# Weight-sum steps of VectorE asked ahead of the norms, and w2 steps that take the block stored first

## The chip, the cores and the metric

The kernel runs on one core of one Trainium2 chip. The metric is device time in microseconds, measured on the chip; every execution that the comparisons use is of the same (fast) state. Waits, stretches and timelines are those of one profiled execution of each kernel. The kernel before takes 1542.65 us (median of three runs, 1542.54 to 1543.26).

## The reference, cut to what matters

Two layers, each an attention with a short dilated window and a gated feed-forward, over 2048 tokens of width 1024. Both layers use the same weights.

```python
def _A_ref(x, wqkv, wo):            # 32 heads of 32, W = 8, dilation 2
    ... q, k, v from x @ wqkv; each token looks at itself and 7 earlier ones ...
def _B_ref(x, w1, w3, w2):          # F = 3584
    gate = jnp.einsum("bsd,df->bsf", x, w1)
    up = jnp.einsum("bsd,df->bsf", x, w3)
    h = _silu(gate) * up
    out = jnp.einsum("bsf,fd->bsd", h, w2)
    return out

x = A_x
x = x + _A_ref(_layernorm(x, axis=-1), A_wqkv, A_wo)
x = x + _B_ref(_layernorm(x, axis=-1), B_w1, B_w3, B_w2)
x = x + _A_ref(_layernorm(x, axis=-1), A_wqkv, A_wo)
x = x + _B_ref(_layernorm(x, axis=-1), B_w1, B_w3, B_w2)
```

## The kernel before

The tokens are worked in blocks of 512. The feed-forward of layer 0 does its first two blocks with plain products. Beside those it builds **weight sums**: ScalarE copies scaled pieces of w1, w3 or w2 into one of two staging blocks in `big`, VectorE adds and subtracts them, GpSimd stores the block to DRAM. All later feed-forward blocks read these sums back and need seven products where plain ones need eight (the scheme of Strassen).

VectorE's order is chosen while the program is built. It keeps queues of small steps, and `background` fills the time until the next fixed piece of work. The step that can start first by its estimate wins, and at a tie the queue that is asked first:

```python
def background(until):
    while True:
        best = None
        for queue in (norms, makes, adds, values, scores):
            step = head(queue)
            if step is not None:
                start = max(now["dve"] + 0.3, step[1])
                if start - 0.3 + step[0] <= until and (best is None or start < best[0]):
                    best = start, queue
        ...
```

The norms' steps are statistics and the application of the norm; each application is followed by a DMA transpose on the sync queue. `makes` holds the weight-sum steps: four VectorE steps for a block, then its stores.

Lines of the kernel before that return below: L841 is a product of Q, K, V, and L845 its evacuation (ScalarE copies a finished product out of PSUM); L712 loads wqkv; L277 is the norm's DMA transpose; L1086 is one of the seven products of the later feed-forward blocks, L1110 VectorE's sum behind it; L1394 adds to the residual. The granted clock is the share of full speed that TensorE was allowed.

```python
def differences(m, g, a, slot, r):            # sums of w1 and w3
    b = blocks[slot]
    for out, x, y in ((4, 5, 1), (1, 1, 0), (2, 4, 0), (6, 3, 2)):
        yield 0.40, r, lambda: nc.vector.tensor_tensor(b[:, out], b[:, x], b[:, y], ...)   # L928
    pending[slot] -= 1
    nc.gpsimd.dma_start(t_d[m][g][:, 4 * a:4 * (a + 1)], b[:, 0:4])                        # L931
    nc.gpsimd.dma_start(t_d[m][g][:, 8 + 3 * a:8 + 3 * (a + 1)], b[:, 4:7])                # L932
    stored[slot] = now["dve"] + 7.0

def sums_of_w2(i, f, ws, loaded):
    a = f % 2
    while "at" not in got2 or pending[a]:
        yield "blocked"
    pending[a] += 1
    b = big[:, a * 3584:(a + 1) * 3584].rearrange("p (b c) -> p b c", b=7)
    for j, (fh, hh) in ((0, (0, 0)), (2, (0, 1)), (1, (1, 0)), (5, (1, 1))):
        yield 0.61, max(loaded, stored[a], got2["at"]), lambda: nc.scalar.activation(      # L1043
            b[:, j], ws[hh][fh][:, f, :], ACTF.Copy, scale=up2[:])
    ...
    def rest():
        ... four VectorE steps ...                                                         # L1049
        pending[a] -= 1
        nc.gpsimd.dma_start(t2_d[i][:, :, f, :], b)                                        # L1052
        stored[a] = now["dve"] + 7.0
```

## Time and profile before

| | kernel before |
|---|---|
| time, median of 3 | 1542.65 us |
| span of the profiled execution | 1542.1 us |
| TensorE busy | 1521.5 us, 99% |
| TensorE busy from 500 to 600 us | 93.11 of 100 us |
| TensorE waits from 100 to 500 us | none listed |
| TensorE waits from 500 to 575 us | 6.8 us |
| TensorE waits from 575 us to the end | 5.8 us |

How to read it: 99% busy says that TensorE is the bound, and that there is little to win. The same number hides where the missing part stands. So the share is read by stretches, and the stretch that stands out is then looked at engine by engine; the prediction does this, with the lines.

### The profile page before, as it was taken

How to read it: one execution, taken by the hardware profiler on the slowest of the kernel's cores; microseconds unless marked ns; L12 is line 12 of the kernel's file. 1: busy time of each engine (PE TensorE's matmuls, PEld its weight loads, DVE VectorE, ACT ScalarE, POOL GpSimd, SP SyncE). 2: the span in 40 equal slices, each digit the busy share in tenths (PEclk: the TensorE clock that was granted, in tenths of full speed). 3: DMA queues.
4: the chain of work that ended last, by engine and by line, in shares of the span. 5: the costliest groups of instructions: out<-in, count | busy, mean ns of one | idle time of the engine just before them, and what ended most of it. 6: DMA issues, size and time to landing. Idle time of an engine off the chain costs nothing.

```text
span 1542.1 us, 25098 instructions
## 1 busy us (share of the span) xinstructions
PE 1521.5 (99%) x9595; PEld 990.2 (64%) x9634; DVE 1200.9 (78%) x2126; ACT 884.8 (57%) x1388; POOL 156.8 (10%) x308
## 2 busy tenths in 40 slices
PE   9999999999999999999999999999999999999999
PEld 7666644444444567675685756867677667686865
DVE  4689998889979678989898958799688986445345
ACT  3885476667465346555574554666557345554633
POOL 1210102121111100102101010010202000000000
PEclk9999999999999999999999999999999999999999
DMA  9887969798896899969879888798979988878885
GB/s 326 192 230 211 271 209 337 266 307 268 270 307 226 289 326 316 313 236 312 294 285 310 310 282 270 268 342 295 308 259 322 347 281 285 311 273 333 313 295 205
DMA packets 261433, 439.57 MB, mean 285 GB/s; under 512 B 73856, under 2 KB 201088, under 8 KB 245056
## 3 DMA queue, kind: packets, MB, share of 16 engines
q1 hardware_dynamic: 248464, 390.90, 77.2%
q0 software_dynamic: 12704, 46.93, 8.7%
q8 instruction: 75, 1.23, 0.3%
q14 instruction: 46, 0.38, 0.1%
q10 hardware_dynamic: 144, 0.13, 0.0%
HBM read 345.90 MB, written 67.90 MB: 268 GB/s over the span
## 4 chain that ended last, share of the span: by engine, by line
PE 55%; DVE 4%; DMA 3%; ACT 3%; issue 1%; POOL 1%; ACTq 0%; DVEq 0%; POOLq 0%
PE st L1086 29%; PE w L1235 15%; PE ps L841 6%; PE po L776 4%; DMA qkv_d<-hT 1%; DMA t_d<-big 1%; DMA kT<-qkv_d 1%; DVE tree L595 1%; DMA xnT<-xn 1%; DVE tree L515 1%; ACT sg L1297 0%; DVE tree L670 0%; ACT big L1043 0%; ACT xn L323 0%; ACT L1297 0%
## 5 line engine op out<-in xcount | busy, mean ns | idle before, releaser
L841 PE MATMUL ps<-xnT,wqkv 128*128 128x512 f16 (+1 forms) x1469 | 320.7, 379 | 3.1 <-ACT hT L845 1.8
L1086 PEld LDWEIGHTS <-early 128*128 128x128 f16 x2688 | 263.1, 98 | 39.9 <-DVE big L303 1.7
L841 PEld LDWEIGHTS <-wqkv 128*128 128x128 bf16 x1472 | 210.6, 144 | 111.6 <-issue 4.0
L1235 PE MATMUL w<-t,hT 128*128 128x512 f16 x1008 | 226.3, 379 | 1.5 <-ACT big L1255 1.2
L1086 PEld LDWEIGHTS <-late 128*128 128x128 f16 x2016 | 197.4, 98 | 33.8 <-issue 5.5
L595 DVE TENSOR_TENSOR tree<-qT,kT 128x2048 bf16<-128x2048 bf16 x128 | 156.2, 1221 | 29.0 <-DMA qT<-qkv_d 15.4
L670 DVE TENSOR_TENSOR tree<-At,vT 128x2048 bf16<-128x2048 bf16 x128 | 156.1, 1220 | 26.8 <-DMA At<-E 25.2
L515 DVE TENSOR_TENSOR tree<-tree 128x1024 bf16<-128x1024 bf16 x256 | 175.2, 685 | 0.9
L1086 PE MATMUL st<-big,early 128*128 128x256 f16 x1344 | 172.8, 273 | 1.9 <-DVE big L303 1.4
L1086 PE MATMUL st<-xnT,late 128*128 128x256 f16 x1344 | 174.2, 273 | 0.2
L1235 PEld LDWEIGHTS <-hT 128*128 128x128 f16 x1008 | 98.3, 98 | 113.6 <-issue 3.1
L1086 PE MATMUL st<-xnT,early 128*128 128x256 f16 x1344 | 165.3, 273 | 0.0
L1098 ACT COPY st<-st 128x512 f32<-128x512 f32 x84 | 48.3, 575 | 119.6 <-PE st L1086 118.8
L776 PE MATMUL po<-wo,oT 128*128 128x512 bf16 x487 | 111.6, 379 | 2.9 <-DVE x_sb L781 1.6
L1358 PE MATMUL pu<-xnT,w3t 128*128 128x512 f16 x448 | 105.8, 379 | 0.0
L1349 PE MATMUL pg<-xnT,w1t 128*128 128x512 f16 x448 | 105.8, 379 | 0.0
L1380 PE MATMUL acc<-w2t,hT 128*128 128x512 bf16 x437 | 97.8, 379 | 0.6
L1110 DVE TENSOR_TENSOR st<-st,big 128x512 f32<-128x512 f32 x84 | 58.4, 695 | 50.2 <-ACT big L1107 50.1
L845 ACT CAST hT<-ps 128x512 bf16<-128x512 f32 x96 | 54.9, 586 | 71.3 <-PE ps L841 70.2
L1297 ACT ACTIVATE sg<-st,down_scale 128x512 bf16<-128x512 f32 x126 | 86.7, 688 | 12.6 <-PE st L1086 12.1
L1086 PE MATMUL st<-big,late 128*128 128x256 f16 x672 | 87.9, 274 | 3.8 <-DVE st L1110 3.8
L776 PEld LDWEIGHTS <-oT 128*128 128x128 bf16 x512 | 50.0, 98 | 58.3 <-issue 2.6
(167 smaller groups left out, 1919.3 us busy)
## 6 DMA issues: line engine op xcount, KB each, us to landing
early<-t_d SPq DMA_DIRECT2D x84, 1024.0 KB, 6.9
late<-t_d SPq DMA_DIRECT2D x84, 768.0 KB, 6.4
t<-t_d SPq DMA_DIRECT2D x42, 1024.0 KB, 7.6
t<-t_d SPq DMA_DIRECT2D x42, 768.0 KB, 5.3
wqkv<-in_A_wqkv_dram SPq DMA_DIRECT2D x28, 1024.0 KB, 9.0
w1t<-in_B_w_dram SPq DMA_DIRECT2D x14, 1024.0 KB, 8.0
w3t<-in_B_w_dram SPq DMA_DIRECT2D x14, 1024.0 KB, 10.9
t_d<-big POOLq DMA_DIRECT2D x28, 512.0 KB, 6.0
```

Source lines behind the costliest of these rows:

```text
L515: nc.vector.tensor_tensor(b, b, buf[:, 4:8, :], op=ALU.add)
L595: V.tensor_tensor(pr, qT[:], kT[:, :, k0:k0 + TCH], op=ALU.mult)
L670: V.tensor_tensor(tm.rearrange("p w (a e) -> p w a e", a=4), At[:].rearrange("p a w e -> p w a e"), win, op=ALU.mult)
L776: nc.tensor.matmul(ps[:], lhsT=oT[:, t, j * P:(j + 1) * P], rhs=wo[:, t, hh * 512:(hh + 1) * 512], start=(t == 0), stop=(t == KT - 1))
L841: nc.tensor.matmul(ps[:], lhsT=ws[kk // KH][:, kk % KH, t::KT], rhs=xnT[:, kk, :], start=(kk == 0), stop=(kk == KT - 1))
L1086: nc.tensor.matmul(out[:, a, :], lhsT=w[:, a, blk, k, :], rhs=rhs[:, k, :], start=start and a == 0 and k == 0, stop=k == KQ - 1, skip_grou ...
L1110: nc.vector.tensor_tensor(G["D"][:], G["D"][:], su, op=ALU.add)
L1235: nc.tensor.matmul(out[:], lhsT=lhs[:, k, j * P:(j + 1) * P], rhs=w[:, k, :], start=start and k == 0, stop=k == nq - 1, skip_group_check=True)
L1297: nc.scalar.activation(sg[:], src, ACTF.Silu, scale=inv)
L1349: nc.tensor.matmul(pg[:], lhsT=w1t[:, kk, fi * P:(fi + 1) * P], rhs=xnT[:, kk, :], start=(kk == 0), stop=(kk == KT - 1))
L1358: nc.tensor.matmul(pu[:], lhsT=w3t[:, kk, fi * P:(fi + 1) * P], rhs=xnT[:, kk, :], start=(kk == 0), stop=(kk == KT - 1))
L1380: nc.tensor.matmul(acc[:], lhsT=hT[:, f, j * P:(j + 1) * P], rhs=tiles[hh][f // nq][:, f % nq, :], start=(f == 0), stop=(f == f1 - f0 - 1))
```

## The change

The intent: weight-sum steps win ties against norm steps, so that blocks are sent to DRAM sooner; and a w2 step takes whichever free block was stored first, not a fixed one. The diff also takes out a version of the V product that nothing called.

```diff
@@ background
-            for queue in (norms, makes, adds, values, scores):
+            for queue in (makes, norms, adds, values, scores):
@@ sums_of_w2
-        a = f % 2
-        while "at" not in got2 or pending[a]:
+        while "at" not in got2 or all(pending):
             yield "blocked"
+        a = min((i for i in range(2) if not pending[i]), key=lambda i: stored[i])
         pending[a] += 1
@@ (cut: dead code goes: v_products, size_of_v, sums_of_v, their tiles and DRAM
@@  buffers, and a third entry in blocks, pending and stored that only they used)
```

More of the change, by code (lines that the diff above doesn't have):

```diff
@@ L217 @@
     size2 = const.tile([P, 16], FP32, name="size2")
-    size_v = const.tile([P, 4], FP32, name="size_v")
-    down_v = const.tile([P, 1], FP32, name="down_v")
-    up_v = const.tile([P, 1], FP32, name="up_v")
     total = const.tile([P, 1], FP32, name="total")
@@ L226 @@
     h16 = hT[:].bitcast(FP16)
-    blocks += [hT[:, 9:16, :].bitcast(FP16).rearrange("p b (k c) -> p b k c", k=KT // 2)]
     t2_d = [dram.tile([P, 7, (b - a) // 2, 512], FP16, name=f"t2_d{i}") for i, (a, b) in enumerate(fsplits)]
     t_d = [[dram.tile([P, 14, KT // 2, P], FP16, name=f"t_d{m}_{g}") for g in range(NG)] for m in range(2)]
-    t_d += [[dram.tile([P, 14, KT // 2, P], FP16, name=f"t_dv_{g}") for g in range(2)]]
     qkv_d = [[dram.tile([P, KT, S], BF16, name=f"qkv_d{l}_{i}") for i in range(3)] for l in range(2)]
@@ L854, in q_part @@
             if l == 0:
-                stored[0:2] = landed, landed
+                stored[:] = landed, landed
             if first and t0 == SG:
@@ L917, in weight_sums, with differences @@
                     scale=up_scale[:, m, g:g + 1])
-            makes.append([differences(m, g, a, a, now["act"] + 0.1), None])
+            makes.append([differences(m, g, a, now["act"] + 0.1), None])
         made.add((m, g))
-    pending, stored, made, held = [0] * 3, [0.0] * 3, set(), []
+    pending, stored, made, held = [0] * 2, [0.0] * 2, set(), []
     junk = hsum[:].bitcast(BF16).rearrange("p k t -> p (k t)")
-    def differences(m, g, a, slot, r):
-        b = blocks[slot]
+    def differences(m, g, a, r):
+        b = blocks[a]
         for out, x, y in ((4, 5, 1), (1, 1, 0), (2, 4, 0), (6, 3, 2)):
@@ L929, in differences @@
                 b[:, out], b[:, x], b[:, y], op=ALU.add if (x, y) == (4, 0) else ALU.subtract)
-        pending[slot] -= 1
+        pending[a] -= 1
         nc.gpsimd.dma_start(t_d[m][g][:, 4 * a:4 * (a + 1)], b[:, 0:4])
         nc.gpsimd.dma_start(t_d[m][g][:, 8 + 3 * a:8 + 3 * (a + 1)], b[:, 4:7])
-        stored[slot] = now["dve"] + 7.0
-    got_v = {}
-    def size_of_v(i, w):
-        w_ = w[:].rearrange("p k c -> p (k c)")
-        half = w_.shape[1] // 2
-        for j in range(2):
-            yield 1.95, 40.0, lambda: nc.scalar.activation(junk, w_[:, j * half:(j + 1) * half], ACTF.Square,
-                                                           accum_out=size_v[:, 2 * i + j:2 * i + j + 1])
-        if i == 1:
-            total_scale(size_v, up_v, down_v, got_v)
-    def sums_of_v(ws):
-        while "at" not in got_v or norm_left.get(("Q", 0, NCH - 1), 1):
-            yield "blocked"
-        for g in range(2):
-            for a in range(2):
-                while pending[2]:
-                    yield "blocked"
-                pending[2] += 1
-                b = blocks[2]
-                for i, (kh, fh) in ((0, (0, 0)), (1, (0, 1)), (3, (1, 0)), (5, (1, 1))):
-                    t = 4 * g + 2 * fh + a
-                    yield 0.61, max(got_v["at"], stored[2]) + 1.0, lambda: nc.scalar.activation(
-                        b[:, i], ws[kh][:, :, t::KT], ACTF.Copy, scale=up_v[:])
-                makes.append([differences(2, g, a, 2, now["act"] + 1.0), None])
-        made.add("v")
+        stored[a] = now["dve"] + 7.0
     def finish_sums(done):
@@ L1152, in pipeline @@
             done(i)
-    def v_products(l, c):
-        key = ("Q", l, c)
-        slots, landed = [0], []
-        def stage(G, pair):
-            if ("to", pair) not in G:
-                i = slots[0] % 8 * SG
-                slots[0] += 1
-                G["to", pair] = hT[:, i:i + SG, :]
-                G["left", pair] = 2
-            return G["to", pair]
-        def consume(G, q, src, r):
-            pair, t0 = q % 2, HT * (q // 2)
-            to = stage(G, pair)
-            if q != 3:
-                nc.scalar.activation(to[:, :, t0:t0 + HT], src, ACTF.Copy, scale=down_v[:])
-                r = act(0.57, r)
-            G["left", pair] -= 1
-            G["at", pair] = max(r, G.get(("at", pair), 0.0))
-            if not G["left", pair]:
-                t = 4 * G["g"] + 2 * pair
-                nc.sync.dma_start(qkv_d[l][2][:, t:t + SG, c * CH:(c + 1) * CH], to)
-                landed.append(dma(256, G["at", pair]))
-                if len(landed) == 4:
-                    qkv_at[l, c, 2] = max(landed)
-        groups = []
-        for g in range(2):
-            G = dict(m=2, g=g, inv=down_v[:])
-            G["corner"] = lambda G=G: stage(G, 1)[:, :, HT:CH]
-            groups.append(G)
-        pipeline(key, groups, consume, lambda i: between(False, i == 0), True)
-        xnT_free[key] = now["pe"]
     def products(u, f0, f1, hold):
@@ L1399, in b_stage @@
         if u == TU - 1:
-            force(makes, lambda: not any(pending[0:2]))
+            force(makes, lambda: not any(pending))
             scale_h()
```

## The prediction

> **What bounds the kernel now.** I read the page first, then busy time by stretch, then what TensorE waited for, and then the timelines of the other engines where TensorE stood still.
>
> ```profile
> PE 1521.5 (99%) x9595; PEld 990.2 (64%) x9634; DVE 1200.9 (78%) x2126; ACT 884.8 (57%) x1388; POOL 156.8 (10%) x308
> 400.00:500.00 100.00, 99.68 (x468) 45.43 (x472) 85.81 (x174) 58.19 (x86) 16.02 (x28) 1.00 0.85 284
> 500.00:600.00 100.00, 93.11 (x581) 65.42 (x582) 74.52 (x133) 47.54 (x79) 7.57 (x12) 0.98 0.90 306
> 1400.00:1500.00 100.00, 100.00 (x761) 74.29 (x760) 45.21 (x70) 48.39 (x78) 0.00 (x0) 1.00 0.88 323
> PE st L1086 <- DVE st L1110: 3.8, 1, 3.8
> PE ps L841 <- ACT hT L845: 1.8, 1, 1.8
> PE ps L841 <- DMA wqkv<-in_A_wqkv_dram: 1.2, 2, 1.0
> 570.00:574.00 4.00, 4.00 (x25) 3.08 (x25) 4.00 (x7) 2.33 (x4) 0.00 (x0) 0.65 0.43 177
> 574.00:578.00 4.00, 4.00 (x39) 3.59 (x38) 3.85 (x8) 2.33 (x5) 0.00 (x0) 1.00 0.68 223
> ```
>
> Columns of the stretches: length, then PE, PEld, DVE, ACT, POOL busy us (instructions), granted clock, DMA share, GB/s. The reader is to see that TensorE bounds the kernel almost everywhere: from 40 to 1500 us it is busy over 97% of every stretch of 100 us, but for one, 500 to 600 us, where 6.9 us are missing. The three wait lines are all that TensorE waited for between 500 and 575 us: 3.8 + 1.8 + 1.2 = 6.8 us. The same view gives no wait at all from 100 to 500 us, and 5.8 us in small pieces from 575 us to the end. The change doesn't touch a matrix product, so it can only be worth what is in such holes. The last two stretches show a cost behind the 3.8 us hole: with the clock at 0.65, 25 matmuls were done in 4 us where the next 4 us did 39, so some (39 - 25) x 0.109 = 1.5 us more were lost (0.109 us is the spacing of these 128x256 products, 8 in 0.87 us).
>
> What makes this hole? It stands where the second block of layer 0's feed-forward ends, the last one that makes weight sums, and Q, K, V of layer 1 begin. The timelines of VectorE, GpSimd, ScalarE and SyncE there:
>
> ```profile
> 491.83 0.42 DVE L928 TENSOR_TENSOR big<-big 128x512 f16<-128x512 f16 x1 [0.39 <-ACT big L915]
> 493.37 0.75 DVE L928 TENSOR_TENSOR big<-big 128x512 f16<-128x512 f16 x2
> 498.95 0.42 DVE L928 TENSOR_TENSOR big<-big 128x512 f16<-128x512 f16 x1
> 502.80 0.41 DVE L928 TENSOR_TENSOR big<-big 128x512 f16<-128x512 f16 x1
> 504.57 1.17 DVE L928 TENSOR_TENSOR big<-big 128x512 f16<-128x512 f16 x3
> ...
> 497.65 0.22 POOL L251 TENSOR_SCALAR rstd<-mv 128x2 f32<-128x2 f32 x1 [2.46 <-DVE mv L249]
> 499.91 0.61 POOL L932 DMA_DIRECT2D t_d<-big  x1 [1.24 <-issue]
> 505.82 0.61 POOL L931 DMA_DIRECT2D t_d<-big  x1
> ...
> 513.99 5.01 ACT L1043 ACTIVATE big<-w2t,up 128x512 f16<-128x512 bf16 x8 [19.08 <-DMA wqkv<-in_A_wqkv_dram]
> 523.83 2.56 ACT L1043 ACTIVATE big<-w2t,up 128x512 f16<-128x512 bf16 x4 [4.83 <-DMA t_d<-big]
> ...
> 526.42 1.68 DVE L1049 TENSOR_TENSOR big<-big 128x512 f16<-128x512 f16 x4 [5.71 <-ACT big L1043]
> ...
> SPq L712 <- ACT big L1043: 9.5, 2, 9.4
> ```
>
> Columns: start, length, engine, line, what; in brackets the idle time before it. The eight last weight-sum steps (L928, 0.42 us each, 3.2 us of work) take from 491.8 to 505.7 us, because norm statistics and norm applications stand between them. So the second of the two blocks is sent off only at 505.8 us. ScalarE then idles 19 us before the first w2 step. The page names a wqkv load, but the matmuls of that stretch run from earlier tiles; I read the semaphores: the one it waited for last was raised at 513.8 us by the store issued at 505.82 us. That follows from the code: step f takes block f % 2, the first step here has f = 3, and block 1 is just the one stored last. Three steps over two blocks then end at 526.4 us. ScalarE, in order, evacuates Q, K, V products only after that (the 1.8 us wait), and the four wqkv loads wait for the w2 tiles it still reads (9.4 us, then the 1.2 us wait). VectorE idles 5.7 us, starts the norm sums and the attention late, and its backlog delays the sum that TensorE needs at 566 us (the 3.8 us).
>
> **What the Trainium skill says.** "TensorE: Matmul & The Clock Gate", Part 1, What's actually happening: after an idle window of about 3.4 us the array runs at half clock until it has been busy about as long. The trace agrees: the 3.80 us gap is the only one so long, and 0.65 follows it. The same page (Architectural detail) says that ScalarE and VectorE queues are strictly first-in first-out, so an emission order decides what waits behind what; the trace agrees, the evacuations start at 526.30, right behind the last w2 step. "DMA: Bandwidth & Descriptors", Anatomy of one DMA: about 2.0 us plus bytes / 436e3 us for a GpSimd-issued one, that is 4.1 us for an 896 KB w2 block; the trace has 4.9 us median for these.
>
> **The change, part by part.** (1) Dead code goes: nothing called the Strassen version of V, so its tiles and DRAM buffers cost no time. I count 0. (2) Weight-sum steps are asked before norms; at equal start times the first queue asked wins. Built and compared engine by engine, the new program has the same instructions in a new order from the first feed-forward block on. At the end of the second block the eight L928 steps stand as two unbroken fours, one before and one after the first residual addition (L1394) of the last half, and the norm statistics follow. (3) The w2 step takes the free block with the earliest store. Compared with the order change alone, this alters little else than some 25 VectorE rows at just this place; there the last four L1049 steps come before the second-last residual addition, where before ten of twelve came after the last. GpSimd's rstd steps no longer split the weight stores.
>
> Worked out at the hole (estimates from the rows above): ScalarE's last L915 ends at 492.35 + 2.56 = 494.9, four L928 take 1.6 us, so block 1 is sent off at about 497 rather than 505.8; block 0 (third and fourth step now adjacent) at about 494 rather than 499.9. A weight store took up to 8.0 us here (505.82 to 513.8), so the blocks are free at about 502 and 505. The w2 steps: block 0 at 502 to 504.5 (4 x 0.62), block 1 at 505 to 507.5, block 0 again after 1.7 us of VectorE and 4.9 us of store, at 511 to 513.6. So they end at about 513.6 rather than 526.4, 13 us earlier, before Q, K, V begin at 514.15. Then ScalarE is free for the first evacuation at 516: -1.8. The wqkv loads go at 514.5 rather than 524.6: -1.2. VectorE gets about 12 us ahead, its gather of scores stands after 80 rather than 120 products of QKV, and the backlog at 566 us should be gone: -3.8, and with it the slow clock: -1.5. Sum: **-8.3 us**. The matmuls do not change, and the last two feed-forward blocks have the same TensorE order in both programs, so what is gained in the middle stays gained.
>
> **The rivals.** First: a new wait in the same place. Norm applications for the next block now come some 5 us later (before about 506 us, after about 511), and their transposes share the sync queue with the wqkv loads; VectorE would stand in order at an L1049 if the third store is late. Six PSUM banks give TensorE about 6 x 1.73 = 10 us of slack, so I expect 0 to 3 us back. It would leave 1537. Second: the whole later schedule of attention moves, and the 5.8 us of small waits after 575 us are dealt anew; VectorE is 90% busy from 700 to 900 us, so it could become 2 or 10. That is 1530 to 1539. Third: the earlier blocks. With norms delayed in the first feed-forward block, the second could start late; but TensorE shows no wait from 100 to 500 us, and the norm steps still stand well before the block's end, so I expect nothing; if wrong, +3 to +6, some 1540. Fourth: the transfers, not VectorE, set the end of the w2 steps (DMA share is 0.90); then only half of the 8.3 comes.
>
> **Range and chances.** -8.3, with 1.3 given back for the first rival and nothing for the second: -7.0, so 1535.6. The second and third rivals make the width: 1529.5 to 1541.5. Over 2% faster would need 31 us, more than all waits of TensorE together (12.6 us after 100 us): 0.01. Over 2% slower would need a new stall of 31 us in an order that keeps every product: 0.02.
>
> **What would show it.** Right: 500 to 600 us with at most 2 us missing from TensorE; last w2 store at about 515 rather than 528.6; the L1043 idle of 19 us cut to below 8; no stretch with clock 0.65 in the middle. Wrong: the wait for L1110 still there though the w2 steps end early (then it is the attention loads that delay VectorE), or new waits after 575 us of more than 6 us beyond the old ones, or waits in 100 to 500 us.

## The result, and the profile after

The changed kernel takes **1532.26 us** (median of four runs, 1531.39 to 1534.33), beside 1542.95 us (1542.54 to 1544.27) for the kernel before. The ratio is 0.9931, with a 95% interval of 0.9914 to 0.9948. A ratio here is the mean time of one kernel's fast runs over that of the other's of the same rounds, so not quite the ratio of the medians quoted. In this kernel the line numbers are lower: L928 is now L923, L1043 is L1009, L1049 is L1015, L1052 is L1018, L1086 is L1052, L712 is L707, L303 is L298.

From the page, busy time; then stretches (columns as in the prediction); then all that TensorE waited for from 580 us on. From 500 to 580 us that view lists nothing.

```profile
PE 1518.1 (99%) x9594; PEld 989.5 (65%) x9634; DVE 1201.8 (78%) x2126; ACT 884.1 (58%) x1388; POOL 153.7 (10%) x308
500.00:600.00 100.00, 99.84 (x635) 69.56 (x637) 87.61 (x152) 49.78 (x80) 8.12 (x13) 1.00 0.88 295
570.00:574.00 4.00, 4.00 (x39) 3.58 (x37) 3.97 (x10) 2.84 (x5) 0.00 (x0) 1.00 0.78 277
PE st L1052 <- ACT big L1073: 2.2, 1, 2.2
PE st L1052 <- ACT sg L1227: 1.1, 1, 1.1
PE w L1165 <- ACT big L1185: 0.5, 1, 0.5
PE st L1052 <- ACT st L1064: 0.4, 1, 0.4
```

The hole is closed: 99.84 us of 100 are busy where it was 93.11, and the stretch at 570 us has a full clock and 39 matmuls where it had 0.65 and 25. What TensorE still waits for adds up to 4.2 us.

The timelines of VectorE, GpSimd, ScalarE and SyncE at the place of the old hole:

```profile
488.10 1.68 DVE L923 TENSOR_TENSOR big<-big 128x512 f16<-128x512 f16 x4
490.82 1.67 DVE L923 TENSOR_TENSOR big<-big 128x512 f16<-128x512 f16 x4
489.84 0.54 POOL L926 DMA_DIRECT2D t_d<-big  x1 [8.19 <-DVE big L923]
492.56 0.54 POOL L926 DMA_DIRECT2D t_d<-big  x1 [1.66 <-DVE big L923]
496.04 2.56 ACT L1009 ACTIVATE big<-w2t,up 128x512 f16<-128x512 bf16 x4 [5.53 <-DVE x_sb L1324]
506.70 2.56 ACT L1009 ACTIVATE big<-w2t,up 128x512 f16<-128x512 bf16 x4 [3.44 <-DMA t_d<-big]
512.91 0.98 POOL L1018 DMA_DIRECT2D t_d<-big  x1 [1.55 <-issue]
506.05 12.03 SPq L272 DMA_TRANSPOSE xnT<-xn  x4
518.18 2.69 SPq L707 DMA_DIRECT2D wqkv<-in_A_wqkv_dram  x4
```

The reader is to see that the eight weight-sum steps stand in two unbroken fours, 488.1 to 492.5 us, where they were spread from 491.8 to 505.7. Everything behind them moves ahead: the last weight-sum block is sent at 492.56 and not at 505.82 us, the w2 steps end at 509.3 and not at 526.4, the last w2 store leaves at 512.91 and not at 528.63, the four wqkv loads at 518.18 and not at 524.58.

To see where the 10.7 us arise, I counted weight loads of TensorE in both traces and took the time at which each kernel reaches the same one. Between the kernels this difference is 0.0 us at the start of Q, K, V of layer 1 (514 us), -9.2 us at the start of the next block's Q, K, V (710 us before, 700 us after), and -11.1 us at the end. So 9.2 us come from the stretch with the hole, and some 2 us from behind it, where the listed small waits fell from 5.8 to 4.2 us.

### The profile page after: what moved, and what is told of

It is laid out like the page before. It is cut to its first block, busy times and chain, and to the rows that moved or that the text cites. A ratio compares the mean times of both kernels' runs of the same rounds, so it can differ in the third digit from the quotient of the medians.

```text
span 1531.0 us, 25095 instructions
## 1 busy us (share of the span) xinstructions
PE 1518.1 (99%) x9594; PEld 989.5 (65%) x9634; DVE 1201.8 (78%) x2126; ACT 884.1 (58%) x1388; POOL 153.7 (10%) x308
## 4 chain that ended last, share of the span: by engine, by line
PE 97%; ACT 1%; issue 1%; DVE 0%; DMA 0%; SPq 0%; ACTq 0%
PE st L1052 32%; PE ps L836 21%; PE w L1165 16%; PE po L771 7%; PE pg L1279 6%; PE pu L1288 6%; PE acc L1310 6%; PE pq L444 1%; PE L L604 0%; DMA wqkv<-in_A_wqkv_dram 0%; ACT L629 0%; ACT L1227 0%; ACT E L629 0%; ACT sg L1227 0%; DVE x_sb L1150 0%
## 5 line engine op out<-in xcount | busy, mean ns | idle before, releaser
L1052 PEld LDWEIGHTS <-early 128*128 128x128 f16 x2688 | 262.6, 98 | 40.4 <-issue 3.5
L1052 PEld LDWEIGHTS <-late 128*128 128x128 f16 x2016 | 197.2, 98 | 30.6 <-issue 2.5
L1052 PE MATMUL st<-xnT,late 128*128 128x256 f16 x1344 | 174.2, 273 | 2.2 <-ACT big L1073 2.2
L1052 PE MATMUL st<-big,early 128*128 128x256 f16 x1344 | 172.3, 273 | 1.6 <-ACT sg L1227 1.1
L1052 PE MATMUL st<-xnT,early 128*128 128x256 f16 x1344 | 165.7, 273 | 0.0
L665 DVE TENSOR_TENSOR tree<-At,vT 128x2048 bf16<-128x2048 bf16 x128 | 156.2, 1221 | 11.9 <-DMA At<-E 10.7
L1052 PE MATMUL st<-big,late 128*128 128x256 f16 x672 | 87.1, 273 | 0.0
```

Of the source, the lines that this page charges most:

```text
L665: V.tensor_tensor(tm.rearrange("p w (a e) -> p w a e", a=4), At[:].rearrange("p a w e -> p w a e"), win, op=ALU.mult)
L1052: nc.tensor.matmul(out[:, a, :], lhsT=w[:, a, blk, k, :], rhs=rhs[:, k, :], start=start and a == 0 and k == 0, stop=k == KQ - 1, skip_grou ...
```

## The experiments

Two theories at first. **A**: the order is what counts; the late weight-sum steps delay everything behind them. **B**: the choice of block has a good share, since the w2 step waited for just the block that was stored last. A third, **C**, came out of the first runs. Each run was timed beside the kernel before on the same chip; that kernel's medians in the four batches were 1544.06, 1543.80, 1544.31 and 1543.96 us.

### First batch: each part alone

**order_only**: the kernel before with one edit.

```diff
-            for queue in (norms, makes, adds, values, scores):
+            for queue in (makes, norms, adds, values, scores):
```

> Only the queue order is changed (weight-sum steps asked before norms); step f still takes block f % 2, so at the end of the second block the first w2 step still waits for the block stored last. Theory A (mine: two causes in one chain, either one alone shortens it): block 1 is sent off at about 493 instead of 505.8 us, lands at about 501, three w2 steps end at about 514 instead of 526.4 us; the wait for the last evacuation and the slow clock go; 8 us less, 1534 +- 2. Theory B (the block choice is what counts, the order only deals the schedule anew): the hole stays, 1540 to 1543.

Measured: 1534.18 us (1533.79 to 1534.84), ratio 0.9935, interval 0.9920 to 0.9949. What TensorE waited for from 500 to 585 us; ScalarE's first two w2 steps; the four wqkv loads and the last w2 store:

```profile
PE st L1086 <- DVE st L1110: 1.3, 1, 1.3
PE ps L841 <- DMA wqkv<-in_A_wqkv_dram: 0.5, 1, 0.5
499.44 5.01 ACT L1043 ACTIVATE big<-w2t,up 128x512 f16<-128x512 bf16 x8 [10.03 <-DMA t_d<-big]
515.67 3.70 SPq L712 DMA_DIRECT2D wqkv<-in_A_wqkv_dram  x4
516.43 0.93 POOL L1052 DMA_DIRECT2D t_d<-big  x1 [4.23 <-ACT hT L845]
```

Of the 3.8 us wait 1.3 are left, and the clock stays full behind them. ScalarE still idles 10 us for the block stored last, and it costs nearly nothing. The order alone gives nearly the whole gain. The last two lines matter for theory C below: here too a w2 store leaves among the four loads, which take 12.3 us to land (median), and yet TensorE waits only 0.5 us for them.

**slot_only**: the kernel before with the other edit. The blocks of the last three w2 steps (f = 3, 4, 5) are swapped, from 1, 0, 1 to 0, 1, 0. The expectation says that nothing else moves; the traces do not bear that out. Up to 508.4 us the engines do the same work in the same order; then the first w2 step's four VectorE steps (L1049) stand at 508.5 us, where they were at 516.6, and VectorE's order differs from there on, ScalarE's from 538.7 us on, both until about 1100 us.

```diff
-        a = f % 2
-        while "at" not in got2 or pending[a]:
+        while "at" not in got2 or all(pending[0:2]):
             yield "blocked"
+        a = min((i for i in range(2) if not pending[i]), key=lambda i: stored[i])
```

> Only the block choice is changed; norms still come first. Built, this gives the same instruction order as the kernel before with the parity flipped for the last three w2 steps alone, so it acts at one place only. Theory A: the stores of the last weight sums are as late as before (499.9 and 505.8 us), so block 0 is free at about 508 and three steps end at about 520 instead of 526.4 us: TensorE does not wait for ScalarE (1.8 us gone), the wqkv wait shrinks, of the 3.8 us and 1.5 us of clock most goes; 1536.5 +- 2. Theory B: all of the gain, 1531 to 1533.

Measured: 1545.91 us (1545.16 to 1548.00), ratio 1.0012, interval 0.9997 to 1.0027. A miss for both theories. The first w2 step does start early, in pieces from 497.9 us on, and the last one ends at 524.3 us, 2 us sooner than before. Yet TensorE waits longer. Its longest wait and the stretch after it; then the last w2 step, the last two w2 stores and the loads:

```profile
PE ps L841 <- DMA wqkv<-in_A_wqkv_dram: 6.7, 2, 4.8
536.00:540.00 4.00, 3.93 (x10) 1.60 (x11) 3.59 (x6) 0.59 (x1) 0.00 (x0) 0.50 1.05 394
521.77 2.56 ACT L1043 ACTIVATE big<-w2t,up 128x512 f16<-128x512 bf16 x4 [3.01 <-DMA t_d<-big]
521.60 0.90 POOL L1052 DMA_DIRECT2D t_d<-big  x1 [9.93 <-DVE big L1049]
522.51 3.30 SPq L712 DMA_DIRECT2D wqkv<-in_A_wqkv_dram  x4
526.57 0.89 POOL L1052 DMA_DIRECT2D t_d<-big  x1 [4.06 <-ACT hT L845]
```

The wqkv loads leave 2 us earlier than in the kernel before, but between two w2 stores, and the tile that TensorE needs is there only at 536 us. The clock is at half for 6.8 us, of which 1.3 still lie in the 4.8 us gap. The first w2 store, at 510.8 us, falls onto two norm transposes in flight: they land 16.4 and 15.2 us after they were issued, where the same two took 9.4 and 8.4 us in the kernel before. The view of transfers shows the medians; from 500 to 540 us, number, KB and median us from issue to landing, first in the kernel before:

```profile
wqkv<-in_A_wqkv_dram SPq DMA_DIRECT2D x6, 1024.0 KB, 9.2
t_d<-big POOLq DMA_DIRECT2D x3, 896.0 KB, 4.9
xnT<-xn SPq DMA_TRANSPOSE x4, 6.3
```

and in slot_only:

```profile
wqkv<-in_A_wqkv_dram SPq DMA_DIRECT2D x6, 1024.0 KB, 12.9
t_d<-big POOLq DMA_DIRECT2D x3, 896.0 KB, 9.7
xnT<-xn SPq DMA_TRANSPOSE x4, 9.7
```

All three kinds take longer. The Trainium skill, "DMA: Bandwidth & Descriptors", Issuing engines are not separate DMA queues, says that transfers from the sync and GpSimd queues run on the same 16 engines and interleave there; these lines agree, since the same bytes land 3 to 5 us later here. This is **theory C**: what counts is where the w2 stores fall, against the transposes and the loads that TensorE waits for.

**both_dead_code_kept**: both edits, the dead code left in.

> Both live changes made on the kernel before, the unused Strassen-V code with its tiles and DRAM buffers kept. The instruction order is that of the changed kernel; only addresses differ. If dead code costs nothing: 1531 to 1534, the time of the changed kernel. If the addresses matter: between that and the time before.

Measured: 1532.98 us (1531.91 to 1534.09), ratio 0.9929, interval 0.9912 to 0.9945, and the waits of the changed kernel. The dead code costs nothing.

**order_first_unit_only**: the new order in the first feed-forward block alone (`stage[0]` is set to the block's number).

```diff
-            for queue in (norms, makes, adds, values, scores):
+            for queue in ((makes, norms) if stage[0] == 0 else (norms, makes)) + (adds, values, scores):
```

> The new queue order in the first feed-forward block alone, the old one elsewhere; block choice as before. The end of the second block then stands as before (eight weight-sum steps split by norms, first w2 step in the block stored last). Theory A: the hole stays and the time is that before, 1541 to 1544. Rival (the gain comes from earlier weight sums all along): half the gain or more, below 1538.

Measured: 1543.88 us (1543.10 to 1544.53), ratio 0.9997, interval 0.9982 to 1.0012. The hole stands: TensorE waits 3.1 us for L1112 (L1110 before), 1.8 us for wqkv and 1.7 us for the evacuation. So the gain is made in the second block.

### Second batch: where in the second block, and which block to take

**order_last_stage**: the new order only from the last w2 stage of the second block on.

```diff
+            for queue in ((makes, norms) if stage[0] else (norms, makes)) + (adds, values, scores):
...
+            stage[0] = u == 1 and lastsplit
```

> The new queue order only from the last w2 products of the second block on (from about 486 us), old before and in it; block choice as before. The last five weight-sum steps then stand unbroken, but one norm application comes behind all w2 steps. Theory A (what counts is when the last two weight blocks are sent off): block 1 is sent off at about 497 us, steps end at about 517, no evacuation wait, hole 1 to 4 us, 1534 to 1538. Rival (the order is needed all through the second block): 1541 to 1544.

Measured: 1539.17 us (1538.08 to 1540.36), ratio 0.9968, interval 0.9952 to 0.9985: half of the gain, just past the upper end of what was expected. The weight-sum stores leave by 497.2 us. What is left is mainly a wait for wqkv, with the clock low behind it:

```profile
PE ps L843 <- DMA wqkv<-in_A_wqkv_dram: 1.9, 1, 1.9
532.00:536.00 4.00, 4.00 (x18) 1.62 (x11) 0.69 (x1) 0.55 (x2) 0.00 (x0) 0.57 1.05 380
```

**last_stored**: the changed kernel with `max` in place of `min`, so that it takes the free block that was stored last, the wrong one on purpose.

```diff
-        a = min((i for i in range(2) if not pending[i]), key=lambda i: stored[i])
+        a = max((i for i in range(2) if not pending[i]), key=lambda i: stored[i])
```

> The changed kernel with the opposite choice: of two free blocks the one stored last. Theory A: with the weight stores issued by 493 us even the wrong block is free at about 501, steps end at about 513 us, before QKV begins: hole below 2 us, 1532 to 1535, as with the order alone. Theory B (the choice decides): the hole comes back, 1540 or more.

Measured: 1534.52 us (1533.60 to 1535.91), ratio 0.9941, interval 0.9922 to 0.9960, with no wait of TensorE from 500 to 585 us. Once the order is changed, even the worst choice of block costs no more than some 2 us. It is not the choice alone, though: the order of work differs from the changed kernel's as well, and the four wqkv loads leave at 508.71 us, before two of the transposes, where they leave at 518.18 us in the changed kernel.

**slot_moved_stores** and **before_moved_stores** test C: slot_only and the kernel before, with two of the last three w2 stores (f = 3 and 5) sent from steps of the first block instead. They are wrong on purpose, since these pieces then hold other data (the record marks these runs as correct all the same; no run tells why).

```diff
-            nc.gpsimd.dma_start(t2_d[i][:, :, f, :], b)
+            for at in {0: (0, 3), 1: (1, 5), 3: (), 5: ()}.get(f, (f,)) if i == 1 else (f,):
+                nc.gpsimd.dma_start(t2_d[i][:, :, at, :], b)
```

> The block choice alone, as in the run of it, but the stores of the first and third w2 step of the last stage (issued there at 510.8 and 526.6 us) are made in the first feed-forward block instead, from other steps' blocks: the bytes are the same, the result is wrong on purpose. Theory C (the earlier steps' stores collide with the norm transposes and the wqkv loads): transposes land by about 519 instead of 523 us, the wqkv waits of 6.7 us fall below 2.5, no half clock after them, 1533 to 1538. Rival (transfers don't matter, it is the order on VectorE or ScalarE): wqkv waits stay above 5 us, 1543 or more.

> The kernel before with the same two stores moved away (wrong on purpose). The third w2 step then needn't wait for the first one's store: steps end at about 521.5 instead of 526.4 us. Theory A: the evacuation wait of 1.8 us goes, the wqkv wait too, of the 3.8 us and its 1.5 us of slow clock at least half: 1535 to 1540. If only the first wait of 19 us matters: 1541 to 1544.

Measured: 1540.31 us (1538.92 to 1541.03), ratio 0.9974, interval 0.9958 to 0.9990; and 1544.06 us (1541.63 to 1545.20), ratio 0.9998, interval 0.9980 to 1.0016. Both are misses in time: the first lies between the ranges of C and of its rival, the second at the upper edge of "only the first wait of 19 us matters". At the hole they do what C says: of TensorE's waits from 500 to 585 us, 0.5 us are left where slot_only had 8.0, and 2.1 us where the kernel before had 6.8; neither has a half clock there. But both have a new wait for w3 near 460 us (2.9 and 2.1 us), with a half clock behind it, and reach Q, K, V of layer 1 more than 5 us late, so the totals say little.

### Third and fourth batch: the same test with the stores elsewhere

To get a total without that loss I sent the two stores at quieter times: near 378 us (**slot_stores_quiet**, **before_stores_quiet**), and, when that too made waits, during Q, K, V of layer 0 (**slot_stores_early**, **before_stores_early**; planned for 130 and 142 us, in the traces near 121 and 140 us). Their outputs are wrong, which doesn't matter for the times. The edit of the last pair; the first pair does the same behind the 16th weight-sum block:

```diff
+                at, s0 = {31: (3, 0), 34: (5, 3)}.get((c * 3 + which) * KT // SG + t0 // SG, (0, 0))
+                if at:
+                    nc.gpsimd.dma_start(t2_d[1][:, :, at, :],
+                                        big[:, 1024 * s0:1024 * s0 + 3584].rearrange("p (b c) -> p b c", b=7))
...
-            nc.gpsimd.dma_start(t2_d[i][:, :, f, :], b)
+            if (i, f) not in ((1, 3), (1, 5)):
+                nc.gpsimd.dma_start(t2_d[i][:, :, f, :], b)
```

> The choice of block alone (instruction order of slot_only), but two of its last three w2 stores, those of the first and third step (f = 3 and 5), are sent at another time: as two stores of the same 896 KB behind the 16th pair of weight stores, near 378 us, where the DMA share by stretch falls to 0.77 and then to 0. Wrong on purpose: those two w2 pieces get other contents. It repeats slot_moved_stores, whose extra stores had been put where a w3 load then landed late (near 460 us), at a quieter place. Theory C (the stores of the w2 steps collide with the norm transposes and the wqkv loads): no TensorE wait over 1 us at 500 to 585 us for wqkv, no half clock there, none near 380 or 460 us either; about 7 to 9 us faster than slot_only, so 1535 to 1539. Rival (the collision is with something else, or the +1.2 us of slot_only came from elsewhere): the 4.8 us wait for wqkv stays, time 1543 to 1546.

> The kernel before with the same two w2 stores sent near 378 us instead. Wrong on purpose. If the hole of the kernel before is made by the late weight-sum steps alone, its first waits stay and about half of it goes with the third step's wait for its store: 1537 to 1541. If transfers made the hole all by themselves, it goes whole: 1535 to 1537. If stores play no part: 1543 to 1545.

> As slot_stores_quiet, but the two moved w2 stores (896 KB each) go out during Q, K, V of layer 0, near 130 and 142 us, where the DMA share is 0.3 to 0.5 and no weight is loaded that TensorE waits for soon; the feed-forward blocks then hold two stores fewer and none more. Wrong on purpose: they carry other data. Theory C (in slot_only the w2 stores of 500 to 530 us collide with the norm transposes and the wqkv loads): no TensorE wait over 1 us from 100 to 585 us, no half clock in the middle, and now in the total too: 1534 to 1538. Rival (removing those stores is worth nothing in all): 1542 to 1546.

> The kernel before with the same two stores moved to 130 and 142 us. Wrong on purpose. The waits for L1110 (3.8 us) and the half clock behind it go, a wqkv wait of 1 to 2 us is left, nothing new arises before 500 us: 1535 to 1539. If the late weight-sum steps make the hole without the stores: 1541 to 1545.

Measured: slot_stores_quiet 1542.68 us (1542.20 to 1543.12), ratio 0.9989, interval 0.9974 to 1.0004, a miss. before_stores_quiet 1544.72 us (1543.60 to 1547.37), ratio 1.0008, interval 0.9990 to 1.0025, a miss: the range of "stores play no part". slot_stores_early 1539.20 us (1538.32 to 1539.27), ratio 0.9962, interval 0.9947 to 0.9977, 1 us past the range of C. before_stores_early 1541.50 us (1539.39 to 1542.74), ratio 0.9981, interval 0.9964 to 0.9997, past the range too, and just inside that of "the late weight-sum steps make the hole without the stores". So no total of the six runs lies in the range that was expected if the stores make the loss. The waits of TensorE, slot_stores_early from 500 to 585 us:

```profile
PE ps L841 <- DMA wqkv<-in_A_wqkv_dram: 0.4, 1, 0.4
```

and before_stores_early from 100 to 500 us (slot_stores_early waits there too, 4.7 us in all):

```profile
PE pu L1363 <- DMA w3t<-in_B_w_dram: 2.2, 1, 2.2
```

The 6.7 us for wqkv of slot_only have shrunk to 0.4, but before 500 us something is lost again. So I took every run apart at three points, by the same count of weight loads as above: how late (+) or early (-) its profiled execution reaches them, against the kernel before.

| run | at Q, K, V of layer 1 | at the next Q, K, V | between the two | at the end |
|---|---|---|---|---|
| the changed kernel | 0.0 | -9.2 | -9.2 | -11.1 |
| order_only | -1.1 | -8.1 | -7.0 | -10.0 |
| slot_only | +0.2 | +2.9 | +2.8 | +1.3 |
| slot_moved_stores | +5.3 | -2.4 | -7.7 | -4.0 |
| slot_stores_quiet | +9.0 | +0.8 | -8.2 | -0.7 |
| slot_stores_early | +5.0 | -2.8 | -7.8 | -4.6 |
| before_moved_stores | +5.4 | -0.9 | -6.3 | -0.7 |
| before_stores_quiet | +6.7 | -0.2 | -6.9 | -0.3 |
| before_stores_early | +3.2 | -4.6 | -7.7 | -4.8 |

The fourth column shows that the two stores matter. With them gone from there, all six runs win 6.3 to 8.2 us between the two points, nearly what the change wins, with the old queue order and whichever block is taken. In the traces the order of work on VectorE, ScalarE and GpSimd is the same in the three slot runs as in slot_only, and in the three before runs as in the kernel before. Nor did their late start help: counted from the start of Q, K, V, the last weight-sum store leaves 7.5 us ahead in the kernel before and 7.5 to 8.4 us ahead in the six. The second column is the price: wherever the stores were put, 3 to 9 us are lost before Q, K, V begin.

It does not show that they matter by collision. A block whose store is gone is also free at once: the third w2 step no longer waits for it (4.83 us in the kernel before, 3.01 us in slot_only). Counted from the start of Q, K, V, the w2 steps end at 4.4 to 7.8 us in the six runs, at 12.5 in the kernel before and at 10.2 in slot_only; the first of the four wqkv loads leaves at 2.6 to 6.0, 10.6 and 8.4 us. (order_only has 2.8 and the changed kernel 4.2.) The loads themselves are no faster than in the kernel before: the four take 11.7 us (median) in before_stores_early and 9.7 us there. For the kernel before, then, the traces point to the wait for the block, which is a link of the prediction's own chain; the collision shows most clearly in slot_only, where the four loads take 13.8 us. No run takes away the one and keeps the other.

What makes that loss is **open** in part. It appears near 460 us even where the stores were sent at 121 and 140 us. before_stores_early and the kernel before have the same order of work, but GpSimd's transfers take eight completion semaphores in turn, and two transfers moved ahead shift which semaphore each later one waits on. The traces show what follows next. In the kernel before, slot_only and order_first_unit_only an earlier w2 store leaves near 434 us, 8.9 to 9.0 us after a w3 load was issued, and that load lands after 13.4 to 13.9 us. In all six runs with moved stores the same store leaves only 4.1 to 5.9 us after the load, and the load lands after 15.2 to 15.7 us. ScalarE, which measures these weights, then waits 0.9 to 2.7 us for them (0 to 0.5 us in the three), starts its next w2 steps later, and the next w1 and w3 loads wait for those. That the shifted semaphores let the store go earlier fits all nine traces, but no run tests it, and this link does not account for the whole 3 to 9 us.

No version was found that beats the changed kernel. In it TensorE waits 4.2 us in all from 580 us on; 3.3 of them are two waits, 1.1 us at 668.0 and 2.2 us at 987.6 us. Just before each, ScalarE switches its function table twice, to the exponential of the attention and back (two loads of 1.28 us each, at 665.19 and 667.10 us and at 984.19 and 986.10 us). That is outside this change.

## Why the prediction was right

Predicted 1535.6 us and the same within 2%; measured 1532.26 us, inside the range of 1529.5 to 1541.5. Its steps in turn:

- **Dead code counts 0**: shown by both_dead_code_kept.
- **The hole gives 8.3 us**: all three waits and the slow clock went. The waits are 6.8 us. The half clock lasted 3.41 us, but its first 0.6 us lie in the gap; the other 2.8 us at half speed cost 1.4 us, so the prediction's 1.5 was well sized. Together 8.2, and the count of weight loads gives 9.2 for the stretch; about 1 us of it has no listed wait.
- **The w2 steps end at 513.6 us**: they end at 509.3. The step that was off is the start of the chain: the estimate had the two blocks sent at about 494 and 497 us, the trace has 489.84 and 492.56, because the order change pulled the earlier stages of the second block ahead too. order_last_stage, without that, sends them by 497.2 us, as estimated, and wins only half (it keeps the old choice of block and puts one norm application behind the w2 steps, so the send-off is not its only difference). So the hole may have closed as fully as it did partly by luck: the estimated times alone were not shown to be enough.
- **First rival, 1.3 us given back to a new wait**: none was. Left alone, the order gives back 0.5 us to wqkv and leaves 1.3 us of the old wait; with the choice of block as well, nothing. The 1.3 us is one part of the 3.7 us by which the gain was underestimated.
- **Second rival, the small waits after 575 us are dealt anew, counted as nothing**: they fell from 5.8 to 4.2 us, and the lead grows by 2 us behind the hole. This is the other part: 8.3 + 2 is 10.3 of the 10.7 us measured. That the dealing came out this way was luck; the prediction had named 2 to 10 us as possible.
- **Third rival, the earlier blocks**: no wait from 100 to 500 us, as expected.
- **Fourth rival, the transfers set the end**: not in the changed kernel. But the prediction gave no reason for leaving it aside, and slot_only shows it at work: there the w2 steps begin early and end only 2 us sooner.

One reading in the prediction was incomplete. It told the hole as one chain: late sums, the block stored last, late w2 steps, late evacuations and loads. Each link is in the trace. But slot_only takes out the wait for the block stored last and wins nothing (its order of work changed too, as said), and before_stores_early keeps the late sums and wins 7.7 us there. What goes with the gain in the runs is the end of the chain, when the last w2 step ends and the wqkv loads leave, and two things set it: when the weight sums are sent, and that a later w2 step waits for its own block's store, which can land late among transposes and loads. The order change wins because it moves the whole group of stores ahead, to 492.56 to 512.91 us: the wqkv loads leave 5 us after the last of them. That the loads meet no store is not needed for it, since in order_only they do. The choice of block adds about 1 us to it (order_only 0.9935 against both_dead_code_kept 0.9929; the intervals overlap, so that it adds anything is not shown).

## What to carry to other kernels

Where TensorE is 99% busy, look for the one stretch that is not, and read there which chain ends last; a small change of order can then win all of it and no more. Before you take away a wait, look at what the released work will start: here a w2 step that began 16 us earlier sent its store into the transposes in flight, the next stores fell around the loads that TensorE needed, and the time did not move. Compare the order of work in the traces, too, before you call a run a test of one edit. And a transfer moved is not a transfer removed: take the trace apart at fixed pieces of work, so that a gain here and a loss there are seen as two numbers.

## What the Trainium skill lacked or had wrong

- "TensorE: Matmul & The Clock Gate", Why this matters for your kernels, advises against TensorE gaps of more than about 3 us. Here shorter gaps halved the clock as well: 1.9 us in order_last_stage (0.57 in the next 4 us of the view) and 2.2 us in before_stores_early (half clock for 3.41 us). Others of that length did not: 2.0 us in slot_stores_early and 2.2 us in the changed kernel kept a full clock. The page calls its window of activity free-running, so where in the window a gap falls may decide; no run here tests that.
- The same page does not say how long the slow stretch gets when the gap runs on into it. In the clock records of the traces it lasts 3.41 or 6.83 us, and not by the length of the gap: 6.83 us after a gap of 3.10 us in order_first_unit_only, 3.41 us after 3.80 us in the kernel before. It was 3.41 us in the five runs where at most 0.6 us of the gap lay behind the fall of the clock, and 6.83 us in the three where 1.0 us (order_first_unit_only), 1.3 us (slot_only) and 2.0 us (slot_stores_quiet) did.
- "DMA: Bandwidth & Descriptors", Anatomy of one DMA: an estimate from its fit gives about 4.1 us for 896 KB (the 4.1 us in the prediction is the same estimate). The trace has 4.9 us median before, and 9.7 us in slot_only for the same transfers beside transposes and loads. The page has no figure for a store that overlaps loads and transposes of its own core.
- The same page, Issuing engines are not separate DMA queues, says that transfers interleave, but not what that does to DMA transposes: their median landing went from 6.3 to 9.7 us in slot_only, with one w2 store falling among them. It is no fixed price: in the changed kernel two w2 stores also leave among the four transposes, and their median is 6.4 us.
- No page that I read tells what it costs to shift GpSimd transfers among their completion semaphores. 3.2 to 9.0 us were lost before Q, K, V of layer 1 in the runs that moved two stores; one link of it is in the traces (a w2 store that leaves 3 to 5 us closer behind a w3 load, which then lands about 2 us later), the rest stayed open.
